# An attention and mixer kernel whose first feed-forward gate runs by token halves, with some loads and thresholds moved

## The chip, the cores and the metric

The kernel runs on one core of a Trainium2 chip. The metric is the device time of one execution in microseconds (us). PE is TensorE, DVE is VectorE, ACT is ScalarE, POOL is GpSimd and SP is SyncE, whose queue issues nearly all DMAs here.

## The reference, cut to what matters

Four batches of 576 tokens go through an attention with 8 heads of 64, a token and channel mixer, and a gated feed-forward layer. All is float32.

```python
scores = (q @ k.T) / 8
scores = where(scores >= max(scores) - tau, scores, -1e9)
attn = softmax(scores) @ v                       # x: (4, 576, 512)
u = x + (relu(x.T @ w_tok1) @ w_tok2).T          # tokens mixed, per channel
x = u + relu(u @ w_ch1) @ w_ch2                  # 512 -> 1536 -> 512
h = relu(x @ w_in)                               # 512 -> 1024
conv[s] = cw[0]*h[s-1] + cw[1]*h[s] + cw[2]*h[s+1]   # along tokens, per channel
out = (h * sigmoid(conv)) @ w_out                # 1024 -> 512
```

## The kernel before, in words

**Stages.** The program starts with `attention(0)` alone. Then, for each batch b, `dense(b)` (the mixer's channel part and the feed-forward layer) is written together with `attention(b + 1)`. Every matmul of the dense part is made of three float16 passes (high by high, low by high, high by low), so each operand exists as a high and a low half, suffixes _h and _l.

**Attention.** A batch has 4 pairs of heads with 9 tiles each, 36 tiles of 128 queries by 576 keys. For each tile PE makes scores (L562, L567 or L571), DVE takes the negated maximum nm (L583), ACT the exponential (L595), DVE masks with the threshold `thr` (L602), ACT makes the float16 high half (L607) and POOL the low half (L611). A DMA on SP then transposes both (L616), and PE multiplies by v (L626, L629; "PV" below). In batch 0 the tiles live in a ring of four places in `act_t`. In batches 0 and 1, where scores are float32, the threshold is made on DVE (L593); in the later ones on POOL. After the 9 tiles of a pair come the normalization (L642 to L655) and the token mixing: first stage L666, second stage L681 and L686, evacuated to the tiles `u` by ACT (L688) and DVE (L689).

**Dense.** L793 is the channel layer up (12 columns f of 128 channels, two token pieces of 256 and 320), L811 the one down, L844 the feed-forward input layer (8 columns f, the same two pieces). The gate of a column follows once both pieces are in `h`: ACT multiplies by the first tap (L827), DVE adds the other two taps (L829, twice), ACT takes a tanh (L831), DVE multiplies (L832), ACT and POOL make the halves of the result in `act_t` (L833, L834). L867 and L870 are the output layer: five token tiles j, each summed over all 8 columns f.

**Weights.** They come as 512-column pieces during attention(0) and dense(0): a load on SP (L347), then POOL (L382), ACT (L385), DVE twice (L386, L388), and ACT and POOL for the halves (L373, L374). `wstep` advances this chain. Its PSUM bank, 4, is handed to the dense part when the last piece (column 7 of w_out) is converted; until then dense(0) has banks 5 and 6, and one output tile j waits for bank 4.

**What sets the order.** All instructions are first recorded in program order; then the class `Order` writes a fixed order for each engine, a list schedule with its own cost figures, which takes the lowest program number among what is ready. Engines and the SP queue then run strictly in that order. Among its rules is `heels`: a load from DRAM that is written after the n-th transposing DMA may not be issued before transpose n-3, as long as n is at most 36, the number of transposes in attention(0).

Of the kernel before, what the change touches and what calls it, by code (L numbers as in the profile page):

```python
# [20 lines left out]
class Order:  # L21
# [4 lines left out]
    def __init__(self, nc, tc, bank_tile, bufs):  # L26
        self.tc, self.bank_tile = tc, bank_tile
        self.group = {n: g for g, names in self.POOLS.items() for n in names}
        self.bufs = bufs
        self.ins = [i for i in nc.cur_bb.bb.instructions if len(i.outs) and self.area(i.outs[0])]  # L30
        n = len(self.ins)
        self.eng = [str(i.engine).split(".")[-1] for i in self.ins]
        self.dma = [i.opcode in ("DMACopy", "DmaTransposeAnt") for i in self.ins]
        self.before, self.first, self.uses, self.turns = [set() for _ in range(n)], [[] for _ in range(n)], [[] for _ in range(n)], {}
        self.depend()
        self.heels, turned = {}, []
        for x, i in enumerate(self.ins):
            if i.opcode == "DmaTransposeAnt":
                turned.append(x)
            elif self.dma[x] and not self.area(i.ins[0])[9] and self.BEHIND < len(turned) <= self.FIRST:  # L40
                self.heels.setdefault(turned[-1 - self.BEHIND], []).append(x)
        self.after = [[] for _ in range(n)]
        for x in range(n):
            for y in self.before[x]:
                self.after[y].append(x)
# [99 lines left out]

    BEHIND, FIRST = 3, 36
    LAP = {"DVE": 85, "Activation": 103, "Pool": 44}
# [102 lines left out]
def kernel(ctx: ExitStack, tc: tile.TileContext, q, k, v, tau,  # L250
# [178 lines left out]
    def load_taps():  # L429
        if conv_w.dtype == F32:  # L430
            nc.sync.dma_start(taps, conv_w)
        else:
# [6 lines left out]
           for i in range(2)]  # L439
    h_t = [const.tile([P, S + 2], F32, name=f"h{i}") for i in range(2)]  # L440
    for t in h_t:
        V.memset(t[:, 0:1], 0.0)
        V.memset(t[:, S + 1:S + 2], 0.0)
    v_t = [(const.tile([P, 2, 2 * NS + 1, D + 2], F16, name=f"vh{i}"),
# [135 lines left out]
    def exps(i):  # L580
# [11 lines left out]
        else:  # L592
            V.tensor_scalar(out=thr, in0=nm, scalar1=-1.0, scalar2=mtaus[:, 0:1], op0=ALU.mult, op1=ALU.add)  # L593
        e = half(i, 0).bitcast(F32) if i < PER else qk2.tile([P, S], F32, tag="x", name="e", bufs=15)
# [156 lines left out]
    def dense(b):  # L751
# [83 lines left out]

        for f in range(NG):
            if b == 0:
                wstep(2)
            for s0, n in SPL:
# [139 lines left out]
```

## Time and profile before

| | |
|---|---|
| median of 3 runs | 770.74 us (770.47 to 771.9) |
| the profiled execution | 770.83 us, its span 769.0 us |
| busy share of the span | PE 95%, DVE 66%, ACT 59%, POOL 54% |
| dense(0)'s first matmul | 114.66 us from the start |
| dense(1)'s first matmul | 304.36 us |

The span runs from the first to the last instruction. All times below are from the span's start. A row's "idle before" names the engine or DMA that ended the wait. Consecutive instructions of one engine overlap by some tens of ns, so a start may lie before the end of the one ahead. The granted clock is 1.0 at 2.4 GHz and 0.5 at 1.2 GHz.

### The profile page before, as it was taken

The page shows a single profiled execution, that of the slowest core. Times are in us where ns is not written, and L with a number is a line of the kernel's source. Part 1 is how long each engine was busy: PE and PEld are TensorE (multiplying, and loading weights), DVE is VectorE, ACT ScalarE, POOL GpSimd, SP SyncE. Part 2 cuts the span into 40 slices and gives each one's busy share as a digit, 9 for nine tenths or more (in the row PEclk, how much of TensorE's full clock was granted, in tenths as well). Part 3 has the DMA queues.
Part 4 walks back from the last instruction along what each step waited for, and adds up shares of the span by engine and source line. Part 5 has one row for each costly group of instructions (what it writes and reads, how often), then busy time and mean ns, then how long its engine had stood idle before and what let it go on. Part 6 is the DMA issues. An engine that isn't in the chain of part 4 may idle for free.

```text
span 769.0 us, 18598 instructions
## 1 busy us (share of the span) xinstructions
PE 726.8 (95%) x7398; PEld 543.3 (71%) x7398; DVE 511.2 (66%) x914; ACT 452.8 (59%) x927; POOL 417.8 (54%) x463
## 2 busy tenths in 40 slices
PE   7889769999998879999999999999999999999998
PEld 4567557777776646788888766778888766788764
DVE  6989768887789961676867952776866941323470
ACT  6977757776768842575657752665656842211471
POOL 5877689887878960466555840366464830000040
PEclk9999979999999999999999999999999999999999
DMA  8999999999997702579777502588863400000001
GB/s 215 224 182 177 265 228 211 240 213 229 204 237 170 156 15 83 122 134 158 159 140 135 86 15 93 114 148 148 153 118 63 78 29 35 1 1 2 1 1 62
DMA packets 200951, 97.00 MB, mean 126 GB/s; under 512 B 174752, under 2 KB 186784, under 8 KB 200864
## 3 DMA queue, kind: packets, MB, share of 16 engines
q1 hardware_dynamic: 200544, 95.55, 59.8%
q8 instruction: 58, 0.95, 0.5%
q10 hardware_dynamic: 320, 0.26, 0.1%
q14 instruction: 29, 0.24, 0.1%
HBM read 39.35 MB, written 4.72 MB: 57 GB/s over the span
## 4 chain that ended last, share of the span: by engine, by line
PE 67%; DVE 9%; DMA 8%; POOL 5%; ACT 5%; issue 4%; SPq 2%; ACTq 0%; POOLq 0%; DVEq 0%
PE ps L811 17%; PE ps L793 15%; PE ps L867 11%; PE ps L844 7%; PE ps L571 4%; PE ps L626 3%; DMA act_t<-act_t 3%; DVE ct L829 3%; PE ps L666 2%; PE ps L681 2%; PE ps L567 2%; PE ps L629 2%; DMA ld<-in_v_dram 1%; POOL ph L611 1%; DVE nm L583 1%
## 5 line engine op out<-in xcount | busy, mean ns | idle before, releaser
L611 POOL TENSOR_TENSOR ph<-e,ph 128x576 f16<-128x576 f32 x108 | 141.6, 1311 | 105.7 <-ACT ph L607 93.5
L811 PE MATMUL ps<-act_t,wc_h 128*128 128x256 f16 (+1 forms) x768 | 149.9, 286 | 0.0
L583 DVE TENSOR_REDUCE nm<-ps 128x1 f32<-128x576 f32 x144 | 107.6, 748 | 20.0 <-PE ps L571 12.8
L602 DVE SCALAR_TENSOR_TENSOR e<-ps,thr,e 128x576 f32<-128x576 f32 x108 | 87.6, 812 | 49.4 <-ACT e L595 41.4
L834 POOL TENSOR_TENSOR act_t<-ct,act_t 128x576 f16<-128x576 f32 x32 | 46.0, 1438 | 132.2 <-ACT act_t L833 130.8
L793 PE MATMUL ps<-u_h,wc_h 128*128 128x320 f16 (+1 forms) x384 | 109.6, 286 | 0.5 <-DVE u_l L689 0.5
L811 PE MATMUL ps<-act_t,wc_l 128*128 128x256 f16 (+1 forms) x384 | 109.7, 286 | 0.0
L793 PE MATMUL ps<-u_h,wc_l 128*128 128x320 f16 (+1 forms) x384 | 109.5, 286 | 0.0
L793 PE MATMUL ps<-u_l,wc_h 128*128 128x320 f16 (+1 forms) x384 | 109.1, 286 | 0.0
L793 PEld LDWEIGHTS <-wc_h 128*128 128x128 f16 x768 | 75.1, 98 | 21.5 <-issue 2.1
L811 PEld LDWEIGHTS <-wc_h 128*128 128x128 f16 x768 | 75.1, 98 | 21.0 <-issue 2.0
L867 PE MATMUL ps<-wo_h,act_t 128*128 128x512 f16 x256 | 77.3, 383 | 4.2 <-ACT h L820 4.2
L829 DVE SCALAR_TENSOR_TENSOR ct<-h,cw,ct 128x576 f32<-128x576 f32 x64 | 71.8, 1125 | 7.5 <-ACT ct L827 7.2
L844 PE MATMUL ps<-u_h,wi_h 128*128 128x256 f16 (+1 forms) x256 | 73.0, 286 | 3.5 <-ACT h L820 1.9
L607 ACT ACTIVATE ph<-e 128x576 f16<-128x576 f32 x108 | 73.1, 677 | 1.2 <-DVE e L602 0.8
L844 PE MATMUL ps<-u_h,wi_l 128*128 128x256 f16 (+1 forms) x256 | 73.1, 286 | 0.0
L844 PE MATMUL ps<-u_l,wi_h 128*128 128x256 f16 (+1 forms) x256 | 73.1, 286 | 0.0
L768 DVE SCALAR_TENSOR_TENSOR act_t<-ps,act_t 128x256 f16<-128x256 f32 x96 | 43.5, 455 | 43.2 <-ACT act_t L767 42.6
L867 PEld LDWEIGHTS <-act_t 128*128 128x128 f16 x384 | 36.9, 98 | 47.2 <-issue 6.4
L626 PE MATMUL ps<-vh,pt 128*128 128x65 f16 (+1 forms) x1080 | 68.8, 195 | 0.6 <-DVE x L646 0.6
L626 PEld LDWEIGHTS <-pt 128*128 128x128 f16 (+1 forms) x1080 | 61.2, 101 | 8.8 <-issue 5.7
L767 ACT ACTIVATE act_t<-ps 128x256 f16<-128x256 f32 x96 | 39.1, 407 | 47.9 <-PE ps L793 47.1
(123 smaller groups left out, 1670.5 us busy)
## 6 DMA issues: line engine op xcount, KB each, us to landing
st<-in_moe_w_ch_dram SPq DMA_DIRECT2D x24, 512.0 KB, 4.6
ld<-in_v_dram SPq DMA_DIRECT2D x32, 160.0 KB, 3.1
kt<-ks SPq DMA_DIRECT2D x32, 144.0 KB, 2.8
st<-in_moe_w_in_dram SPq DMA_DIRECT2D x8, 512.0 KB, 5.0
st<-in_moe_w_out_dram SPq DMA_DIRECT2D x8, 512.0 KB, 4.4
out_dram<-ot SPq DMA_DIRECT2D x16, 256.0 KB, 2.0
kt<-in_k_dram SPq DMA_DIRECT2D x16, 144.0 KB, 4.1
ld<-in_q_dram SPq DMA_DIRECT2D x8, 288.0 KB, 3.6
```

The costliest lines, as they stand in the source:

```text
L583: V.tensor_reduce(out=nm, in_=c["s3"], axis=AX.XY, op=ALU.max, negate=True)
L602: V.scalar_tensor_tensor(out=e3, in0=c["s3"], scalar=c["thr"], in1=e3, op0=ALU.is_ge, op1=ALU.mult)
L607: A.activation(out=c["ph"][:, 0:S], in_=c["e"], func=AF.Copy)
L611: G.tensor_tensor(out=c["ph"][:, S:], in0=c["e"], in1=c["ph"][:, 0:S], op=ALU.subtract)
L626: T.matmul(dst[o:o + m], pt[:, j, o:o + m], vh[:, hh, j, 0:D + 1], start=(j == 0), stop=(j == NSL - 1))
L768: V.scalar_tensor_tensor(out=r_t(f, 1)[:, sl], in0=t, scalar=0.0, in1=r_t(f, 0)[:, sl], op0=ALU.max, op1=ALU.subtract)
L793: T.matmul(t, wc1[wx][:, f, c], u[c][ux][:, sl], start=(c == 0 and i == 0), stop=(c == NC - 1 and i == 2))
L811: T.matmul(t, wc2[wx][:, c, f], r_t(f, rx)[:, sl], start=(by_dve(c) and f == 0 and i == 0), stop=(f == NF - 1 and i == 2))
L829: V.scalar_tensor_tensor(out=ct, in0=ht[:, kk:kk + S], scalar=cw[:, kk, f:f + 1], in1=ct, op0=ALU.mult, op1=ALU.add)
L834: G.tensor_tensor(out=g_t(f, 1), in0=ct, in1=g_t(f, 0), op=ALU.subtract)
L844: T.matmul(t, wi[wx][:, f, c], u[c][ux][:, s0:s0 + n], start=(c == 0 and i == 0), stop=(c == NC - 1 and i == 2))
L867: T.matmul(t, g_t(f, gx)[:, j * P:(j + 1) * P], wo[wx][:, f], **lim)
```

## The change

Three parts. In `dense(0)` alone, the feed-forward input layer and its gate run by halves of the tokens: all 8 columns for tokens 0 to 287, then all 8 for the rest, with two extra tokens per half for the convolution (290 of PSUM's columns instead of 256 and 320). `h` becomes four buffers of a half instead of two of the whole, and two memsets restore the layout for the other batches. Loads that are written after transposes 31 to 36 wait for transpose 36. The threshold of float32 batches is made by ACT.

```diff
-            elif self.dma[x] and not self.area(i.ins[0])[9] and self.BEHIND < len(turned) <= self.FIRST:
-                self.heels.setdefault(turned[-1 - self.BEHIND], []).append(x)
+            elif self.dma[x] and not self.area(i.ins[0])[9] and self.BEHIND < turned <= self.FIRST:
+                heel = turned - 1 - self.BEHIND if turned <= self.LAST else self.FIRST - 1
+                self.heels.setdefault(turns[heel], []).append(x)
...
-    BEHIND, FIRST = 3, 36
+    BEHIND, LAST, FIRST = 3, 30, 36
...
-            V.tensor_scalar(out=thr, in0=nm, scalar1=-1.0, scalar2=mtaus[:, 0:1], op0=ALU.mult, op1=ALU.add)
+            A.activation(out=thr, in_=nm, func=AF.Identity, scale=-1.0, bias=mtaus[:, 0:1])
...
+        def h_half(f, x, t):
+
+            ht = h_t[f % 2][:, (f // 2 + x) % 2 * HW:][:, :HW]
+            A.activation(out=ht[:, 1:HW - 1], in_=t, func=AF.Relu, scale=1.0 / WS2)
+            ct = qk2.tile([P, S], F32, tag="x", name="ct", bufs=15)[:, :hn]
+            A.activation(out=ct, in_=ht[:, 2 * x:2 * x + hn], func=AF.Copy, scale=cw[:, 0, f:f + 1])
+            for kk in (1, 2):
+                V.scalar_tensor_tensor(out=ct, in0=ht[:, 2 * x + kk:2 * x + kk + hn], scalar=cw[:, kk, f:f + 1], in1=ct,
+                                       op0=ALU.mult, op1=ALU.add)
+            A.activation(out=ct, in_=ct, func=AF.Tanh, scale=0.5 / SX)
+            V.scalar_tensor_tensor(out=ct, in0=ct, scalar=1.0, in1=ht[:, 2 * x + 1:2 * x + 1 + hn], op0=ALU.add, op1=ALU.mult)
+            gh, gl = [g_t(f, y)[:, x * hn:(x + 1) * hn] for y in range(2)]
+            A.activation(out=gh, in_=ct, func=AF.Copy)
+            G.tensor_tensor(out=gl, in0=ct, in1=gh, op=ALU.subtract)
...
+        if b == 0:
+            for x in range(2):
+                for f in range(NG):
+                    wstep(1)
+                    bk = dbank()
+                    s0 = x * (hn - 2)
+                    t = ps[:, bk, :hn + 2]
+                    for c in range(NC):
+                        for i, (wx, ux) in enumerate(PASS):
+                            T.matmul(t, wi[wx][:, f, c], u[c][ux][:, s0:s0 + hn + 2],
+                                     start=(c == 0 and i == 0), stop=(c == NC - 1 and i == 2))
+                    flush()
+                    late.append((bk, lambda f=f, x=x, t=t: h_half(f, x, t)))
+                    yield
```

Line numbers behind the change are larger by 2 or 3 up to the gate and by 33 behind it: L616 is then L619, L829 and L832 become L846 and L849 in the halves, L867 is L900.

The first place is the SP queue at the end of attention(0), where `st` is a piece of weights, `ld` is v, and `qt` and `kt` are q and k of a coming pair of batch 1. Before, from the 28th transpose on:

```order
L616 DMA_TRANSPOSE act_t<-act_t 128x9x128 x4
L347 DMA st<-in_moe_w_ch_dram 128x1024
L513 DMA ld<-in_v_dram 128x320 x2
L616 DMA_TRANSPOSE act_t<-act_t 128x9x128 x4
L347 DMA st<-in_moe_w_ch_dram 128x1024
L473 DMA qt_166<-in_q_dram 128x576
L482 DMA kt_0_167<-in_q_dram 64x576
L616 DMA_TRANSPOSE act_t<-act_t 128x9x128
L528 DMA vh_159<-vh_159 64x2x264
L483 DMA kt_1_168<-in_k_dram 64x2x288
L482 DMA kt_0_167<-in_q_dram 64x576
L483 DMA kt_1_168<-in_k_dram 64x2x288
```

After, from the same transpose on:

```order
L619 DMA_TRANSPOSE act_t<-act_t 128x9x128 x9
L349 DMA st<-in_moe_w_ch_dram 128x1024
L516 DMA ld<-in_v_dram 128x320 x2
L349 DMA st<-in_moe_w_ch_dram 128x1024
L476 DMA qt_170<-in_q_dram 128x576
L485 DMA kt_0_171<-in_q_dram 64x576
L486 DMA kt_1_172<-in_k_dram 64x2x288
L485 DMA kt_0_171<-in_q_dram 64x576
L486 DMA kt_1_172<-in_k_dram 64x2x288
L349 DMA st<-in_moe_w_ch_dram 128x1024
```

Six loads that stood among the last nine transposes (two pieces of weights, two of v, one each of q and k) now stand behind the last one, ahead of three more of k and a piece of weights that stood there before too.

The second place is ACT at the last tiles of attention(0); the copies to float16 from `act_t` to `act_t` are those of the tiles (L607, now L610). Before, down to the last tile's copy:

```order
L607 ACTIVATE act_t<-act_t 128x576
L595 ACTIVATE act_t<-ps,nm 128x576
L671 ACTIVATE rh<-ps 128x256
L607 ACTIVATE act_t<-act_t 128x576
L385 ACTIVATE ps<-st 128x512
L595 ACTIVATE e<-ps,nm 128x576
L688 ACTIVATE u_2_h<-ps 128x256
L595 ACTIVATE e<-ps,nm 128x576
L385 ACTIVATE ps<-st 128x512
L607 ACTIVATE act_t<-act_t 128x576
```

After, over the same tiles:

```order
L596 ACTIVATE thr<-nm,mtaus 128x1
L598 ACTIVATE act_t<-ps,nm 128x576
L610 ACTIVATE act_t<-act_t 128x576
L375 ACTIVATE wc_h<-wf 128x512
L596 ACTIVATE thr<-nm,mtaus 128x1
L674 ACTIVATE rh<-ps 128x256
L598 ACTIVATE act_t<-ps,nm 128x576
L610 ACTIVATE act_t<-act_t 128x576 x2
L387 ACTIVATE ps<-st 128x512
L691 ACTIVATE u_2_h<-ps 128x256
L596 ACTIVATE thr<-nm,mtaus 128x1
```

The last two tile copies are now neighbours. Before, two steps of the weights (L385), two exponentials of batch 1 and an evacuation (L688) lay between them. A threshold now stands ahead of exponentials. Further on, the scaling of `kt` for batch 1's second pair (L490, now L493) stands between the two evacuations of the last tile of u; before, it stood ahead of both.

The third place is DVE around the last piece of weights in dense(0); its two steps are the last L386 and L388 (now L388 and L390), `ct` is a gate's work tile and `h_153` and `h_154` are the two `h` tiles. Before:

```order
L388 SCALAR_TENSOR_TENSOR wf<-st,ps 128x512
L829 SCALAR_TENSOR_TENSOR ct<-h_154,cw,ct 128x576
L829 SCALAR_TENSOR_TENSOR ct<-h_153,cw,ct 128x576
L386 SCALAR_TENSOR_TENSOR ps<-st,ps 128x512
L832 SCALAR_TENSOR_TENSOR ct<-ct,h_154 128x576
L388 SCALAR_TENSOR_TENSOR wf<-st,ps 128x512
L829 SCALAR_TENSOR_TENSOR ct<-h_153,cw,ct 128x576
L643 RECIPROCAL rc<-rc 128x5
L583 TENSOR_REDUCE nm<-ps 128x1
L386 SCALAR_TENSOR_TENSOR ps<-st,ps 128x512
L832 SCALAR_TENSOR_TENSOR ct<-ct,h_153 128x576
L388 SCALAR_TENSOR_TENSOR wf<-st,ps 128x512
```

After:

```order
L846 SCALAR_TENSOR_TENSOR ct<-h_153,cw,ct 128x288
L388 SCALAR_TENSOR_TENSOR ps<-st,ps 128x512
L846 SCALAR_TENSOR_TENSOR ct<-h_153,cw,ct 128x288
L390 SCALAR_TENSOR_TENSOR wf<-st,ps 128x512
L649 TENSOR_TENSOR x_3921<-ps,rc 128x4x64
L849 SCALAR_TENSOR_TENSOR ct<-ct,h_153 128x288
L846 SCALAR_TENSOR_TENSOR ct<-h_154,cw,ct 128x288
L652 SCALAR_TENSOR_TENSOR x_3921<-ps,rc,blk 128x128
L388 SCALAR_TENSOR_TENSOR ps<-st,ps 128x512
L846 SCALAR_TENSOR_TENSOR ct<-h_154,cw,ct 128x288
L390 SCALAR_TENSOR_TENSOR wf<-st,ps 128x512
L849 SCALAR_TENSOR_TENSOR ct<-ct,h_154 128x288
```

Behind the last piece's second step stood 3 of the 24 gate operations of 576 columns; now 7 of the 48 of 288 columns stand there. On PE the output layer's first matmuls (L900) now stand ahead of the last two units of the input layer (L863); before, all of the input layer stood ahead of them.

## Rows read from the trace of the kernel before

**Rows 1.** The page: busy tenths of PE and granted clock in 40 slices.

```profile
PE   7889769999998879999999999999999999999998
...
PEclk9999979999999999999999999999999999999999
```

**Rows 2.** Windows of 3 us: length, busy time by engine (count), clock, DMA, GB/s.

```profile
99.00:102.00 3.00, 0.00 (x0) 0.00 (x0) 0.37 (x3) 1.17 (x3) 2.85 (x3) 0.94 1.58 179
...
105.00:108.00 3.00, 2.25 (x19) 1.39 (x20) 2.72 (x6) 1.73 (x4) 1.33 (x3) 0.50 1.11 287
```

**Rows 3.** Timeline of the SP queue: start, length, line, DMA.

```profile
86.42 0.52 SPq L347 DMA_DIRECT2D st<-in_moe_w_ch_dram  x1
86.99 0.90 SPq L513 DMA_DIRECT2D ld<-in_v_dram  x2
...
95.29 0.54 SPq L347 DMA_DIRECT2D st<-in_moe_w_ch_dram  x1
...
97.03 2.23 SPq L616 DMA_TRANSPOSE act_t<-act_t  x1
```

**Rows 4.** The chain that ended last, in order of time: start, length, what.

```profile
97.03 6.74 DMA act_t<-act_t
...
106.99 3.31 PE ps L666 x30
...
114.66 4.25 PE ps L793 x36
...
287.67 1.68 PE ps L666 x30
289.34 10.37 PE ps L867 x48
...
472.26 2.74 PE ps L870 x48
```

**Rows 5.** The page, DMA issues: count, median us to landing.

```profile
act_t<-act_t SPq DMA_TRANSPOSE x36, 3.7
```

**Rows 6.** Timeline of ACT: the last two tile copies of attention(0).

```profile
90.26 0.68 ACT L607 ACTIVATE act_t<-act_t 128x576 f16<-128x576 f32 x1 [1.14 <-DMA act_t<-act_t]
...
94.20 0.68 ACT L607 ACTIVATE act_t<-act_t 128x576 f16<-128x576 f32 x1
```

**Rows 7.** Timeline of POOL: the last low halves of attention(0).

```profile
89.05 3.75 POOL L611 TENSOR_TENSOR act_t<-act_t 128x576 f16<-128x576 f32 x3
...
95.01 1.28 POOL L611 TENSOR_TENSOR act_t<-act_t 128x576 f16<-128x576 f32 x1 [0.44 <-PE ps L629]
```

**Rows 8.** Groups by line over the span: the thresholds, and a like-sized ACT operation.

```profile
L593 DVE TENSOR_SCALAR thr<-nm,mtaus 128x1 f32<-128x1 f32 x72 | 14.6, 204 | 0.4
...
L588 ACT ACTIVATE bias<-nm 128x1 f32<-128x1 f32 x72 | 14.4, 201 | 45.4 <-DVE nm L583 45.0
```

**Rows 9.** Windows in the gate stage of dense(0), columns as in rows 2.

```profile
268.00:272.00 4.00, 0.85 (x7) 0.49 (x5) 4.00 (x5) 0.68 (x1) 3.37 (x3) 1.00 0.06 12
...
228.00:277.00 49.00, 39.70 (x411) 28.51 (x410) 48.37 (x66) 38.66 (x74) 42.64 (x37) 0.97 0.63 134
```

**Rows 10.** Groups by form on DVE from 228 to 277: the gate.

```profile
L829 DVE SCALAR_TENSOR_TENSOR ct<-h,cw,ct 128x576 f32<-128x576 f32 x14 | 19.5, 1396 | 0.0
L832 DVE SCALAR_TENSOR_TENSOR ct<-ct,h 128x576 f32<-128x576 f32 x7 | 8.2, 1168 | 0.0
```

**Rows 11.** Single lines over the span: durations in ns, minimum, median, maximum.

```profile
L829 DVE SCALAR_TENSOR_TENSOR ct<-h,cw,ct x64: 802/874/1920, 232.8 to 747.1; 128x576 f32<-128x576 f32 x64
...
L776 DVE TENSOR_TENSOR us<-us,u_l x18: 424/491/1414, 357.4 to 709.5; 128x256 f32<-128x256 f32 x9, 128x320 f32<-128x320 f32 x9
```

**Rows 12.** Timelines of DVE, ACT and PE: last weight piece, then dense(1)'s start.

```profile
276.11 0.67 DVE L388 SCALAR_TENSOR_TENSOR wf<-st,ps 128x512 int32<-128x512 int32 x1
...
276.82 0.63 ACT L373 ACTIVATE wo_h<-wf 128x512 f16<-128x512 f32 x1
...
304.36 0.27 PE L793 MATMUL ps<-u_h,wc_h 128*128 128x256 f16 x1
```

More of the change, by code (lines that the diff above doesn't have):

```diff
@@ L35, in __init__ @@
         self.depend()
-        self.heels, turned = {}, []
+        self.heels, turned = {}, 0
+        turns = [x for x, i in enumerate(self.ins) if i.opcode == "DmaTransposeAnt"]
         for x, i in enumerate(self.ins):
             if i.opcode == "DmaTransposeAnt":
-                turned.append(x)
-            elif self.dma[x] and not self.area(i.ins[0])[9] and self.BEHIND < len(turned) <= self.FIRST:
-                self.heels.setdefault(turned[-1 - self.BEHIND], []).append(x)
+                turned += 1
+            elif self.dma[x] and not self.area(i.ins[0])[9] and self.BEHIND < turned <= self.FIRST:
+                heel = turned - 1 - self.BEHIND if turned <= self.LAST else self.FIRST - 1
+                self.heels.setdefault(turns[heel], []).append(x)
         self.after = [[] for _ in range(n)]
@@ L439 @@
            for i in range(2)]
-    h_t = [const.tile([P, S + 2], F32, name=f"h{i}") for i in range(2)]
+    HW = S // 2 + 4
+    h_t = [const.tile([P, 2 * HW], F32, name=f"h{i}") for i in range(2)]
     for t in h_t:
-        V.memset(t[:, 0:1], 0.0)
-        V.memset(t[:, S + 1:S + 2], 0.0)
+        for o in (0, HW - 1, HW, 2 * HW - 1):
+            V.memset(t[:, o:o + 1], 0.0)
     v_t = [(const.tile([P, 2, 2 * NS + 1, D + 2], F16, name=f"vh{i}"),
@@ L834, in gate @@
             G.tensor_tensor(out=g_t(f, 1), in0=ct, in1=g_t(f, 0), op=ALU.subtract)
-        for f in range(NG):
-            if b == 0:
-                wstep(2)
+        def h_half(f, x, t):
[25 more added lines that the diff above has]
+                    yield
+            flush()
+            for t in h_t:
+                V.memset(t[:, S + 1:S + 2], 0.0)
+        for f in range(NG if b else 0):
             for s0, n in SPL:
```

## The prediction

> **What bounds the kernel now.** I read the page's slices first. From slice 16 on (about 307 us) PE is busy nine tenths or more of every slice but the last, at full clock [rows 1], so time can be won there only by taking work from PE, which the change does not do; what is won or lost before 307 us is carried to the end. Ahead of that two places stand out. Around 100 us PE does nothing for three microseconds and then runs at half clock [rows 2]. From 228 to 277 us DVE is busy 48.37 of 49 us and POOL 42.64, while PE has only 39.70; between 268 and 272 PE works 0.85 us [rows 9]. The chain of waits names the first cause: the last transpose of attention(0), 6.74 us long, is followed by the first stage of the token mixing and then by dense(0) [rows 4]. In the second place DVE is the bound; the DVE groups show that the gate is most of it, and that it is slow there: 1396 and 1168 ns for operations whose like takes 802 at least [rows 10, 11]. From 114 to 228 us PE is full again [rows 1], so a lead won at 100 us should reach the gate stage.
>
> I make the sum against the profiled execution, 770.8 us (span 769.0), 0.1 above the median of the runs. A change of less than about 0.2%, 1.5 us, can't be told from none.
>
> **The deferred loads.** The last tile's copy on ACT starts 3.9 us after the one before it [rows 6], because five other operations stand between; with the change they are neighbours. Then POOL is next: it is busy until 92.80 with three low halves, and the last follows at once and ends at 94.1 rather than 96.3 [rows 7]. The transpose was also issued 0.7 us after its data were there (97.03 against 96.29), behind loads that now follow it [rows 3]. So it is issued 2.9 us earlier. Its landing took 6.74 us against a median of 3.7 [rows 4, 5], with a piece of weights and two more loads issued just ahead; without them I take the median, 3.0 us less. From there to dense(0)'s first matmul 10.9 us passed (103.77 to 114.66), part of it at half clock: 30 matmuls of the first mixing stage took 3.31 us, where the same 30 take 1.68 at full clock [rows 4]. If PE's idle stretch shrinks from nearly 5 us to about one, the clock should stay up; that is 1.6 us there and, as an estimate for the scores and the second stage in the same stretch, 0.9 more. Sum: 2.9 + 3.0 + 2.5 = 8.4.
>
> A new wait may take part of it. Nine loads, 2.2 MB, now follow the last transpose, and ACT's evacuation of the last u tile stands behind the scaling of the ninth, a piece of k. At the 179 to 287 GB/s of these windows [rows 2] they need 8 to 12 us from about 95, so they land between 103 and 107; with the scaling and evacuation (some 1.5 us) the second half of u is there at 105 to 109, and it is needed a token piece after dense(0) starts at 106.3. I take **8.0 us** won. Least: only the 0.7 and 3.0, 3.7 us. Most: 8.4 plus what the thresholds give.
>
> **The thresholds.** 72 operations of 204 ns leave DVE, 36 in attention(0); an ACT operation of that size takes 201 [rows 8]. Each overlaps its neighbours by about 0.08 us, so 36 are 4.4 us on either engine. DVE is the busier one there, but ACT's exponential now starts later by one such step, and the mask waits for it. I take zero, with 2 us to either side.
>
> **From dense(0) to the gate.** PE starts dense(0) with 28 PV matmuls fewer done than before (the order); 30 slightly wider ones take 1.68 us [rows 4], so about 1.0 comes back later, and 0.5 for late pieces of weights: **+1.5**. The postponed fourth piece was loaded at 86.42 [rows 3] for the fourth column of dense(0), which came some 10 us after 114.66; now it is loaded at about 95 for a column at about 116, still 20 us ahead.
>
> **The gate by halves.** PE's work is the same (192 matmuls of 290 columns for 96 of 256 and 96 of 320). What it buys: output tiles of the first tokens need only first-half gates. But each tile also sums over all columns of w_out, and the last piece of these is converted on DVE among the gates. It was ready on DVE at 276.79 and its high half on ACT at 277.45 [rows 12]. In the changed order, PE has behind it three matmuls of one output tile, a whole tile, the first mixing stage, two tiles, the half tile and the second mixing stage. From [rows 4]: 0.65 + 5.18 + 1.68 + 10.37 + 2.74, and 1.9 for the rest of the way to 304.36 (289.34 + 10.37 + 2.74 = 302.45); in all 22.5 us. Had DVE kept its time, dense(1) would start at 277.45 + 22.5 = 300.0, a gain of 4.4.
>
> DVE does not keep it. Ahead of the last piece's second step stood 14 + 7 gate operations, 27.7 us [rows 10], less 0.08 overlap each, 26.0. Now 41 halves stand there. Undisturbed, one of 288 columns takes about 0.458 us (between 424 and 492 ns for 256 and 320 [rows 11]). The disturbance, averaged over the 21, is 0.52 us above 0.80. Does a half pay it in full? The short operations of the same sort reach 1414 ns, 0.9 above their least, as the long ones do [rows 10, 11]: it goes by operation, not by length. In full: 41 x (0.458 + 0.52 - 0.08) = 36.8, 10.8 us more than now. In proportion to length, 0.26: 26.2, no more than now. POOL's work is spread over a longer stretch, and its operations on the gate are shorter too, so I take 0.38: 31.1, **5.1 us more**. Six thresholds that leave and two small operations that come in about cancel. So 300.0 + 5.1 = 305.1 against 304.36: **+0.8 us**, bounds -4.3 and +6.5.
>
> The Trainium skill, "SBUF — State Buffer", section "Who interferes with whom", says that VectorE operations with two SBUF inputs and GpSimd operations that read SBUF exclude each other for a whole instruction. By that rule the wait does not shrink with the half; the maxima in [rows 11] agree, and the sum by it is the 10.8 us, which makes it the rival "in full" below.
>
> **Sum.** -8.0 + 1.5 + 0.8 = -5.7: 770.8 - 5.7 = **765.1 us**.
>
> **The rivals.** *The disturbance stays in full* (0.52 per operation): the gate stage loses 6.5, 770.8 - 8.0 + 1.5 + 6.5 = 770.8, no change. For it: the maxima of short operations; against it: the same POOL work in a longer stretch. *Slower: gates that follow each other pair off with POOL's*. The half gates stand closer together in DVE's order, and one that starts while POOL holds an operation of 1.3 us waits for most of it. At 0.70 per operation DVE needs 44.2 us, 18.2 more, the stage loses 13.9, and the time is 778.2. It decides from 0.56 on, where the loss of 8.1 and the 1.5 outweigh the lead with 1.5 to spare. For it: the mean of the 14 longer operations is already 0.59 over their least [rows 10, 11]; against it: POOL is not always busy. *The disturbance is in proportion*: the stage gains 4.3, the time is 760.0. For it: shorter POOL operations between; against it: [rows 11]. *The deferral gives little*: POOL's data come no earlier and the clock falls all the same; 3.7 won, 770.8 - 3.7 + 1.5 + 0.8 = 769.4. For it: the nine loads that now gate the last u tile.
>
> **How the numbers follow.** Forecast 0.45, in proportion 0.18, in full 0.10, slower 0.15, little from the deferral 0.12. Faster by over 0.2%: 0.45 + 0.18 + 0.07 of the last, 0.70. Slower: 0.15. Within: the rest, 0.15. The range reaches from 758 (in proportion, with 2 us from the thresholds) to 771 (in full); the slower rival beyond it and the far end below are left out. The forecast's own range is 762 to 768.5.
>
> **What the changed profile would show.** The last transpose issued at about 94 and landed within 4 us; no stretch at half clock around 105; dense(0)'s first matmul at 106 to 107; in the gate stage 48 gate operations with a mean of about 0.84 us; the last weight piece's second DVE step 5 us later relative to dense(0)'s lead; dense(1)'s first matmul at about 298.7. I am wrong if dense(0) starts after 110, if the half gates take 1.0 us or more, or if PE shows new gaps between 115 and 228, where I count on none.

## The result: 0.8% slower, and where the time went

The changed kernel takes 777.09 us (median of 4 runs, 776.09 to 778.28) against 770.61 for the kernel before beside it (769.77 to 771.9): ratio 1.0083, 95% interval 1.0059 to 1.0106. The forecast was 765.1, faster. The profiled execution is 776.1 us (span 774.3) against 770.8.

The page of the kernel after, busy tenths of PE and granted clock, to be laid beside [rows 1]:

```profile
PE   7788779999998789999999999999999999999998
...
PEclk9999999999999899999999999999999999999999
```

Windows of the kernel after: length, busy time by engine (count), clock, DMA share, GB/s.

```profile
99.00:102.00 3.00, 2.18 (x33) 1.28 (x29) 2.83 (x7) 2.65 (x6) 2.83 (x5) 1.00 0.90 295
105.00:108.00 3.00, 2.61 (x28) 1.90 (x29) 2.32 (x5) 1.64 (x6) 2.75 (x6) 1.00 1.07 210
110.00:113.00 3.00, 1.12 (x9) 0.68 (x8) 1.09 (x2) 2.50 (x6) 1.29 (x2) 1.00 0.74 190
268.00:272.00 4.00, 2.00 (x17) 1.34 (x15) 4.00 (x7) 3.35 (x9) 2.77 (x3) 1.00 0.26 53
228.00:277.00 49.00, 37.67 (x363) 27.36 (x360) 47.11 (x71) 37.00 (x87) 36.65 (x38) 0.91 0.57 134
```

Where PE did nothing for three microseconds and then ran at clock 0.50 [rows 2], it now has 2.18 and 2.61 of 3 us at full clock. A new hole stands at 110 to 113 (1.12 of 3). In the gate stage PE is busy 2 us less (37.67 against 39.70) and has done 363 matmuls there instead of 411, at a clock of 0.91 instead of 0.97; DVE is still busy for nearly the whole of it, and POOL is busy 6 us less [rows 9].

The chain that ended last, kernel after, start, length, what:

```profile
97.36 4.67 DMA st<-in_moe_w_ch_dram
102.05 8.37 DMA kt<-in_k_dram
...
283.85 2.66 DVE ct L846 x3
...
286.96 5.56 PE ps L900 x25
292.52 1.68 PE ps L669 x30
294.20 10.37 PE ps L900 x48
```

The transpose that led the chain at 97.03 [rows 4] is gone from it. In its place stands the deferred load of k, and 180 us later three half gates on DVE; behind them stands an evacuation on DVE (L692) for which the output tiles on PE wait. The last two rows of before, at 287.67 and 289.34, come 4.85 us later now, and the distance from there to the end hardly changes. All of the loss is made ahead of 292 us.

The start of dense(0), timelines of SP, ACT and PE in the kernel after (start, length, operation, idle time before it):

```profile
88.31 9.01 SPq L619 DMA_TRANSPOSE act_t<-act_t  x5
...
96.01 1.30 SPq L619 DMA_TRANSPOSE act_t<-act_t  x1
...
102.05 0.78 SPq L486 DMA_DIRECT2D kt<-in_k_dram  x1
```
```profile
110.50 0.77 ACT L493 ACTIVATE kt<-kt,qsc 128x576 f32<-128x576 f32 x1 [1.97 <-DMA kt<-in_k_dram]
111.18 0.42 ACT L691 ACTIVATE u_h<-ps 128x320 f16<-128x320 f32 x1
```
```profile
108.20 0.27 PE L796 MATMUL ps<-u_h,wc_h 128*128 128x256 f16 x1
...
112.18 0.30 PE L796 MATMUL ps<-u_h,wc_h 128*128 128x320 f16 x1 [1.88 <-DVE u_l L692]
```

The last transpose is issued at 96.01, 1.0 us earlier than before, and its data are there at 99.25, 4.5 us earlier. dense(0) starts at 108.20 instead of 114.50 (the 114.66 of [rows 4] is where the chain enters it). Then PE waits 1.88 us for the second half of the last u tile, whose evacuation stands on ACT behind the scaling of the deferred k, which landed at 110.4.

The gate and its end: groups on DVE from 228 to 294 (count, busy us, mean ns), and the timelines of DVE and PE at the last weight piece and at dense(1)'s start.

```profile
L846 DVE SCALAR_TENSOR_TENSOR ct<-h,cw,ct 128x288 f32<-128x288 f32 x32 | 26.8, 850 | 1.1 <-ACT ct L844 1.1
L849 DVE SCALAR_TENSOR_TENSOR ct<-ct,h 128x288 f32<-128x288 f32 x16 | 12.2, 763 | 1.9 <-ACT ct L848 1.8
```
```profile
282.54 0.68 DVE L390 SCALAR_TENSOR_TENSOR wf<-st,ps 128x512 int32<-128x512 int32 x1
```
```profile
309.21 0.27 PE L796 MATMUL ps<-u_h,wc_h 128*128 128x256 f16 x1
```

A half gate operation takes 0.82 us in the mean; 0.84 was forecast. The last piece's second step starts at 282.54, against 276.11 before, and dense(1) at 309.21 against 304.36 [rows 12].

From the start of the token mixing at about 211 us to dense(1), windows of before, of the kernel after, and of two kernels that follow below, halves_alone and deferral_alone:

```profile
212.81:304.36 91.55, 82.25 (x841) 56.81 (x839) 68.42 (x103) 56.37 (x110) 60.10 (x55) 0.98 0.57 132
211.11:309.21 98.10, 85.84 (x840) 59.13 (x839) 73.43 (x121) 61.93 (x143) 57.91 (x63) 0.95 0.54 122
212.08:307.47 95.39, 84.48 (x840) 58.27 (x839) 73.33 (x130) 59.95 (x134) 57.96 (x63) 0.96 0.54 128
209.15:305.84 96.69, 84.01 (x841) 57.53 (x840) 69.51 (x106) 57.26 (x112) 62.06 (x57) 0.96 0.54 129
```

The same 838 matmuls start in each of the four stretches. Of the 6.6 us that the kernel after needs more, PE is idle for 3.0 and busy for 3.6 more. The granted clock explains most of the busy part: 0.95 of 98.1 us where 0.98 of 91.6 were granted, which makes an estimated 3 us of full-speed time that were not granted. In halves_alone 1.6 are idle and 2.2 busy, in deferral_alone 3.4 and 1.8. No run holds the clock fixed, so the two parts aren't separated by an experiment.

Four moments of each profiled execution carry what follows. "Mixing" is the first matmul of the stage of token mixing at about 211 us, "last piece" the start of the last second step of a weight piece on DVE; all are read from the timelines of PE and DVE. The difference is that of the medians of a kernel and of the kernel before on the same chip, in us; the interval is that of the ratio.

| kernel | difference | interval | dense(0) | mixing | last piece | dense(1) |
|---|---|---|---|---|---|---|
| before | | | 114.50 | 212.81 | 276.11 | 304.36 |
| after | +6.5 | 1.0059 to 1.0106 | 108.20 | 211.10 | 282.54 | 309.21 |
| halves_alone | +4.3 | 1.0034 to 1.0068 | 114.34 | 212.08 | 281.04 | 307.47 |
| deferral_alone | +3.1 | 1.0027 to 1.0059 | 108.39 | 209.15 | 279.78 | 305.84 |
| thr_alone | +3.2 | 1.0026 to 1.0051 | 115.98 | 214.26 | 276.18 | 305.51 |
| no_halves | +1.5 | 1.0006 to 1.0033 | 109.86 | 212.82 | 277.16 | 305.47 |
| no_thr | +3.2 | 1.0028 to 1.0056 | 108.84 | 209.98 | 279.68 | 306.36 |
| no_deferral | +8.0 | 1.0091 to 1.0136 | 116.55 | 214.85 | 283.11 | 310.23 |
| lap_84 | +3.4 | 1.0026 to 1.0060 | 114.08 | 213.40 | 275.19 | 307.52 |
| lap_86 | +1.5 | 0.9992 to 1.0026 | 114.08 | 211.85 | 276.21 | 304.82 |
| deferral_keep_qk | +4.7 | 1.0034 to 1.0073 | 110.72 | 211.01 | 282.41 | 308.46 |
| halves_by_column | +3.9 | 1.0037 to 1.0071 | 114.43 | 211.08 | 279.70 | 306.72 |
| halves_weights_first | +4.1 | 1.0051 to 1.0080 | 116.16 | 212.90 | 264.23 | 307.38 |
| halves_deferral_weights_first | +4.8 | 1.0050 to 1.0095 | 109.35 | 210.25 | 267.78 | 308.01 |
| thr_second | +0.9 | 0.9997 to 1.0025 | 114.80 | 212.42 | 274.80 | 304.30 |
| deferral_thr_second | +3.1 | 1.0027 to 1.0068 | 112.05 | 213.88 | 279.55 | 307.86 |
| all_thr_second | +6.7 | 1.0069 to 1.0106 | 109.61 | 211.86 | 283.59 | 310.75 |
| short_dense | -3.9 | 0.9927 to 0.9968 | 112.93 | | 273.36 | 299.09 |
| low_half_by_act | +0.2 | 0.9985 to 1.0018 | 113.19 | 210.06 | 274.15 | 302.02 |
| short_dense_low_half | -7.1 | 0.9902 to 0.9936 | 113.10 | | 268.93 | 296.44 |

Single runs of one kernel lie several us apart (the kernel before: 766.61 to 773.22 over all of its runs; deferral_thr_second: 770.28 to 777.57). The moments belong to one execution each, so a difference of 1 us between two of them says little. That of before took 770.83 us, about 1 us above its medians beside the experiments (769.56 to 770.02), and that of deferral_thr_second 777.27, 4.5 us above its median.

### The profile page after: what moved, and what is told of

It is laid out like the page before. It is cut to its first block, busy times and chain, and to the rows that moved or that the text cites. A ratio compares the mean times of both kernels' runs of the same rounds, so it can differ in the third digit from the quotient of the medians.

```text
span 774.3 us, 18626 instructions
## 1 busy us (share of the span) xinstructions
PE 731.3 (94%) x7398; PEld 544.3 (70%) x7398; DVE 510.4 (66%) x872; ACT 468.7 (61%) x1023; POOL 415.1 (54%) x471
## 4 chain that ended last, share of the span: by engine, by line
PE 63%; DMA 10%; POOL 7%; ACT 7%; DVE 7%; issue 4%; SPq 2%; POOLq 0%; ACTq 0%; DVEq 0%
PE ps L814 18%; PE ps L900 10%; PE ps L796 10%; PE ps L877 5%; DMA act_t<-act_t 4%; PE ps L629 3%; PE ps L574 3%; PE ps L669 3%; POOL ph L614 2%; PE ps L684 2%; PE ps L570 2%; PE ps L632 2%; DMA ld<-in_q_dram 2%; DMA ld<-in_v_dram 1%; DMA st<-in_moe_w_out_dram 1%
## 5 line engine op out<-in xcount | busy, mean ns | idle before, releaser
L837 POOL TENSOR_TENSOR act_t<-ct,act_t 128x576 f16<-128x576 f32 x24 | 34.4, 1432 | 128.4 <-ACT act_t L836 127.0
L900 PE MATMUL ps<-wo_h,act_t 128*128 128x512 f16 x256 | 76.8, 381 | 3.9 <-ACT h L842 3.0
L610 ACT ACTIVATE ph<-e 128x576 f16<-128x576 f32 x108 | 73.0, 676 | 1.0 <-DVE e L605 0.8
L900 PEld LDWEIGHTS <-act_t 128*128 128x128 f16 x384 | 36.8, 98 | 46.0 <-issue 4.8
L877 PE MATMUL ps<-u_h,wi_h 128*128 128x256 f16 (+1 forms) x192 | 54.9, 286 | 1.3 <-ACT h L823 1.0
L877 PE MATMUL ps<-u_l,wi_h 128*128 128x256 f16 (+1 forms) x192 | 54.9, 286 | 0.0
L877 PE MATMUL ps<-u_h,wi_l 128*128 128x256 f16 (+1 forms) x192 | 54.9, 286 | 0.0
L565 PE MATMUL ps<-kt,qt 128*128 128x288 f32 (+1 forms) x160 | 46.8, 450 | 8.3 <-DVE act_t L605 8.2
```

The lines of the kernel that those rows point to most:

```text
L565: T.matmul(s3[o:o + m, a], f32(st["qt"])[:, q0:q0 + m], f32(st["kt"][hh])[:, a * hn:(a + 1) * hn], start=True, stop=True)
L610: A.activation(out=c["ph"][:, 0:S], in_=c["e"], func=AF.Copy)
L877: T.matmul(t, wi[wx][:, f, c], u[c][ux][:, s0:s0 + n], start=(c == 0 and i == 0), stop=(c == NC - 1 and i == 2))
L900: T.matmul(t, g_t(f, gx)[:, j * P:(j + 1) * P], wo[wx][:, f], **lim)
```

## The experiments

### Each edit alone, and the change without each

The kernel before with one of the three edits (halves_alone, deferral_alone, thr_alone), and the kernel after with one taken back (no_halves, no_thr, no_deferral). Taking back the deferral is one number, and taking back the thresholds one line:

```
-    BEHIND, LAST, FIRST = 3, 30, 36
+    BEHIND, LAST, FIRST = 3, 36, 36
...
-            A.activation(out=thr, in_=nm, func=AF.Identity, scale=-1.0, bias=mtaus[:, 0:1])
+            V.tensor_scalar(out=thr, in0=nm, scalar1=-1.0, scalar2=mtaus[:, 0:1], op0=ALU.mult, op1=ALU.add)
```

What was expected of the first four, then of the other two:

> The kernel before with only the gate of the first batch by halves; loads and thresholds as before. Theory A (the halves cost DVE time, and the last piece of w_out comes later): the gate stage loses what it lost in the changed kernel, about 6.5 us, so 776 to 778 us, with the last w_out piece's second DVE step some 5 to 8 us later than the 276.1 of before, and dense(0) at 114.5 as before. Theory B (the halves are about free and the loss comes from the thresholds on ACT): 769 to 772. Theory C (the three edits only hurt together, because a reshuffled order meets another one): 768 to 772 too, but then each edit alone is within 2 us.

> The kernel before with only the late loads moved behind the last transpose of attention(0). Theory A: dense(0) starts about 6 us earlier (108 to 109 instead of 114.5), 1.9 us go to the wait for the second half of the last u tile behind the k load on ACT, and about 2.5 to score and PV matmuls that come back later, so the lead is 1.5 to 2.5 us and the time 768 to 769. The recorded forecast would have 764 to 765. Theory B: the lead lost between 108 and 211 us was the thresholds' doing, so 765 to 767.

> The kernel before with only the float32 thresholds on ACT (72 operations of 0.28 us there instead of 0.20 on DVE). Theory A: in the first 60 us, where PE waits for DVE's masks, the mask waits for the later exponential, and PE is 1.3 us less busy there; all in all 770 to 772. Theory B: the thresholds are the main loss, 774 to 777. If neither, the freed DVE time shows as a gain, 767 to 769.

> The changed kernel with the gate of the first batch whole again; deferral and thresholds stay. Theory A: the gate stage's loss is gone and the lead of 1.7 us at 211 us carries through, 768 to 770. Theory B: still 774 to 777. Theory C: anything else, above all a time that is not the sum of the two single edits.

> The changed kernel with the float32 thresholds back on DVE: halves and deferral stay. If the losses simply add (halves 4, deferral 3, thresholds 3 us against the kernel before, each alone), 776 to 777. If they are new orders of one and the same gate stage, that don't add, 772 to 776. First mixing stage of dense(0)'s tail at about 209 us, as with the deferral alone.

> The changed kernel with the late loads at their old places: halves and thresholds stay. If the losses add, 776 to 777; if they don't, 771 to 775. dense(0) starts at about 116 us, as with the thresholds alone.

Every edit alone is slower, by 3 to 4 us. None of the theories had said so: theory A had the deferral alone ahead. The parts don't add either. Their sum is 10.5, the whole change costs 6.5, and deferral with thresholds (no_halves) only 1.5. With the halves against without them, the cost is 4.3 (alone), 0.2 (beside the deferral), 4.8 (beside the thresholds) and 5.0 (beside both). The deferral costs 3.1 alone and gives back 1.0 to 1.7 beside the others, of the 8 forecast.

The moments are steadier than the times. The deferral does bring dense(0) forward in all four of these kernels that have it, by 4.6 to 6.3 us against before (in deferral_thr_second, below, by 2.5 only, in an execution far above its median). But deferral_alone, 6.1 us ahead at dense(0) and 3.7 at the mixing, is 1.5 us behind at dense(1): the gate stage, from mixing to dense(1), takes 96.7 us there and 91.6 before. The wait for the last u tile isn't the reason: deferral_alone has none of it (ACT scaled that k at 106.83 there, 3.7 us earlier than in the kernel after). PE waits in the gate stage instead; waits of deferral_alone from 212 to 290 us (us in total, times, longest):

```profile
PE ps L846 <- ACT h L822: 7.6, 3, 5.7
PE ps L569 <- DVE e L604: 1.7, 1, 1.7
```

PE needs a bank of PSUM that ACT has still to evacuate into h. Before the longest of these waits ends, that evacuation stands on ACT behind the copy of an earlier column's gate, which waits 3.03 us for DVE; timeline of ACT, then a row of the chain that ended last (L846 is the input layer in this kernel):

```profile
264.58 0.68 ACT L835 ACTIVATE act_t<-ct 128x576 f16<-128x576 f32 x1 [3.03 <-DVE ct L834]
265.17 0.37 ACT L822 ACTIVATE h<-ps 128x256 f32<-128x256 f32 x1
```
```profile
265.59 5.08 PE ps L846 x20
```

PE had waited 5.7 us, and the granted clock is 0.50 while these 20 matmuls run. They take 5.08 us; at full clock 36 of like size take 4.25 [rows 4], so the lower clock costs about 2.7 us here, as an estimate, on the chain.

### Another order, the same work

One constant of the planner's cost model is changed in the kernel before (lap_84, and lap_86 to the other side). No instruction comes or goes.

```
-    LAP = {"DVE": 85, "Activation": 103, "Pool": 44}
+    LAP = {"DVE": 84, "Activation": 103, "Pool": 44}
```

> A placebo: the kernel before with one constant of its planner changed, the time it reckons a DVE operation to overlap the next, from 85 to 84 ns. No work is added or taken away, only the order that the planner writes changes, as it does after every edit. Theory C (the kernel before is an order tuned by hand, and any new order of the gate stage costs some us): slower by 1.5 to 4 us, with dense(1) later by as much and the loss in the gate stage. Theory A and B (the edits themselves cost): within 1 us of before.

> The same placebo to the other side, 86 ns instead of 85. Theory C: slower by 1 to 4 us. Theories A and B: within 1 us of before.

84 costs 3.4 us, as much as an edit; 86 can't be told from none. Theory C holds in so far that an order alone can cost what one edit does. In lap_84 it is made in the gate stage too: 94.1 us from mixing to dense(1). Windows of lap_84:

```profile
240.00:272.00 32.00, 25.73 (x288) 19.72 (x287) 32.00 (x44) 24.22 (x49) 31.75 (x27) 1.00 0.61 122
272.00:290.00 18.00, 15.33 (x113) 8.41 (x113) 9.46 (x16) 8.47 (x17) 9.92 (x9) 0.81 0.04 15
```

DVE and POOL are full up to 272, and PE then has 2.7 us of idle time and a clock of 0.81. So a loss of 3 us after a single edit is no proof of that edit's own cost; only what recurs in several kernels, or shows in the moments, can be put down to it.

### Does a lead get through the gate stage?

short_dense leaves one of three passes (low half of the weights by high half of u) out of dense(0)'s first layer, so its output is less precise:

```
                     for i, (wx, ux) in enumerate(PASS):
+                        if b == 0 and i == 1:
+                            continue
```

> The kernel before, without the second of the three passes (low half of the weights by high half of u) of dense(0)'s first layer: 96 matmuls of 256 or 320 columns less, about 11.6 us of TensorE's time, so its output is less precise; every operation on DVE, ACT and POOL stays. It gives the gate stage a lead that no reordering has to find. If a lead at 211 us carries through the gate stage, as the forecast took it, dense(1) starts 9 to 11 us earlier and the time is 759 to 761. If the gate stage is bound by the work of POOL and DVE and by the loads of w_out, whenever TensorE gets there, most of it is lost there: 765 to 769.

Of 11.6 us less work on PE, 9.3 are there at the first matmul of the gate's input layer (216.69 against 225.96; dense(0) had started 1.6 earlier), 5.3 at dense(1), and 3.9 in the median. The lead does not get through. The windows of 228 to 272 us, first of short_dense, then of before, and the waits of short_dense in the stage:

```profile
228.00:272.00 44.00, 34.83 (x379) 25.14 (x378) 42.02 (x60) 34.12 (x67) 43.76 (x39) 0.92 0.57 140
```
```profile
228.00:272.00 44.00, 35.73 (x398) 26.97 (x397) 43.42 (x59) 34.15 (x64) 39.09 (x33) 1.00 0.70 149
```
```profile
PE ps L846 <- ACT h L822: 8.1, 4, 3.7
```

POOL has become full (43.76 of 44), DVE nearly so, and PE waits 8.1 us for the same evacuation. Earlier work on PE runs into engines that have no more room.

low_half_by_act takes work from POOL: the low half of each gate of the first batch is a scaled copy by ACT (and not the low half).

```
-            G.tensor_tensor(out=g_t(f, 1), in0=ct, in1=g_t(f, 0), op=ALU.subtract)
+            if b:
+                G.tensor_tensor(out=g_t(f, 1), in0=ct, in1=g_t(f, 0), op=ALU.subtract)
+            else:
+                A.activation(out=g_t(f, 1), in_=ct, func=AF.Copy, scale=2.0 ** -13)
```

> The kernel before, with the low half of each gate of the first batch written by ACT, as a scaled copy, and not by POOL as the difference (eight operations of 1.48 us leave POOL, and its result is not the low half): this takes work from POOL and with it the waits of DVE's gate operations on POOL, and adds eight copies of about 0.7 us to ACT. If POOL with DVE is the bound of the gate stage, the mean of DVE's first gate operations falls from 1.40 to 1.1 us or less, the last weight piece comes 4 to 8 us earlier, and the time is 763 to 767. If not, 768 to 772.

The time stays. DVE's first gate operations fall to 1238 ns from 1396 only, and POOL's busy time from 39.09 to 29.71 of 44 us; now PE waits for attention(1)'s transposes instead:

```profile
PE ps L626 <- DMA pt<-ph: 4.5, 1, 4.5
```

The way from mixing to dense(1) takes 92.0 us, 91.6 before. POOL alone is thus not the bound either. Both probes in one:

> Both probes in one: the kernel before without one pass of dense(0)'s first layer (765.7 by itself) and with the gate's low halves as ACT copies in place of POOL's differences (769.7 by itself); both results are less precise. If the gate stage is held by TensorE's late arrival and by POOL in turn, each hiding the other, the two together give more than their sum: 758 to 762. If it is held by something that neither touches (DVE, the loads of w_out, the order), about their sum or less: 764 to 767.

7.1 us, where the two medians add to 3.7. That speaks for two limits that hide each other. In the profiled executions the gains at dense(1) are 5.3, 2.3 and together 7.9, which is about the sum; but low_half_by_act had its 2.3 at the mixing already. Counted from the first matmul of the gate's input layer to dense(1), the stage takes 78.4 us before, 82.4 in short_dense, 78.8 in low_half_by_act and 78.9 with both: of a lead of 8.4 us at its start (217.53) only 0.5 are lost in it, where short_dense lost 4.0 of 9.3. So in these executions a lead gets through once POOL's gate work, and with it a part of DVE's waits for POOL, is gone. The other 3 us of the 11.6 are lost ahead of the stage.

### Which loads were deferred

deferral_keep_qk lets only weights and v wait for the last transpose; q and k keep their places (the edit against deferral_alone).

```
-                heel = turned - 1 - self.BEHIND if turned <= self.LAST else self.FIRST - 1
+                heel = self.FIRST - 1 if turned > self.LAST and self.area(i.outs[0])[0][:2] not in ("qt", "kt") else turned - 1 - self.BEHIND
```

> The deferral alone, but the loads of q and k for the next attention keep their places; only weights and v wait for the last transpose. If the scaling of the late k on ACT, ahead of the last u tile, is what held dense(0) up, that wait of about 1.9 us at 111 us is gone, but one or two of these loads stand ahead of the last transpose again, so dense(0) starts at 108 to 110. The first mixing stage at 211 us comes at 208 to 209. Theory A says the lead is then kept and the time is 767 to 769; theory C says that the gate stage swallows it as it did with the whole deferral (7 us more from the mixing at 209 us to the last weight piece than before), 771 to 774.

dense(0) starts at 110.72. PE still waits 1.4 us for a u tile, so earlier k loads don't end that wait. From mixing to dense(1) 97.5 us pass, the most of the kernels with whole gates. The gate stage swallows the lead, as theory C had it.

### What in the halves costs

Both start from halves_alone. halves_by_column runs both halves of a column one after the other; halves_weights_first keeps the order of the halves but puts all of the weights' last conversion steps among the first halves. halves_deferral_weights_first is the latter with the deferral.

```
-            for x in range(2):
-                for f in range(NG):
+            for f in range(NG):
+                for x in range(2):
                     wstep(1)
...
-                    wstep(1)
+                    wstep(2 - 2 * x)
```

> The halves alone, but column by column: both halves of a column one after the other, as the whole gates were, with the same 48 half operations on DVE. If the cost of the halves is in the operations themselves (5.7 us more from the mixing at 212 us to the last weight piece), dense(1) starts at 309 to 311 and the time is 775 to 778, since the early output tiles are lost as well. If it is the order of the halves (first all first halves) that costs, it is back at 769 to 772.

> The halves alone, with the last sixteen steps of the weights' conversion all among the first halves of the gate (two to a unit), and none among the second. If the halves lose because the last piece of w_out waits on DVE behind the second halves' operations (281.0 us there, 276.1 in the kernel before), that piece is ready some 6 to 9 us earlier, at 272 to 275, and the time is back at 767 to 770. If the stage is held elsewhere (the second halves themselves, attention(1), loads), dense(1) stays at 306 to 308 and the time at 773 to 775.

> The same with the deferral too. By the first theory the lead of the deferral would be kept as well, 764 to 767; by the other one, 771 to 774, like halves and deferral without the earlier conversion (772.8).

halves_by_column is as slow as halves_alone (3.9 and 4.3), so the order of the halves is not it, though dense(1) did not come to 309 either: losing the early tiles costs nothing that shows. Converting early moves the last piece from 281.04 to 264.23 and leaves dense(1) where it was, 307.38 against 307.47. The place of the last piece, on which the forecast hung the gate stage, does not set its end. Window and waits of halves_weights_first:

```profile
240.00:256.00 16.00, 6.58 (x58) 4.55 (x57) 16.00 (x26) 12.33 (x27) 14.82 (x17) 0.88 0.77 179
```
```profile
PE ps L629 <- DVE x L649: 5.2, 1, 5.2
PE ps L570 <- DVE e L605: 4.3, 2, 3.0
```

With DVE full (16.00 of 16), the conversions that come forward push attention(1)'s operations back, and PE waits for those. It looks as if the whole sum on DVE has to be worked off, whatever stands first: in halves_alone DVE is busy 42.96 of the 44 us up to 272, and it goes on with gates to 286. That is a reading; no run takes work from DVE alone. With the deferral, halves_deferral_weights_first is 4.8 us slower than before: no lead is kept.

Eight kernels of the table have the halves and can be compared with one that lacks only them. The halves cost 3.6 to 5.0 us in six of these pairs, and 0.2 and 1.7 in the two whose other kernel is deferral_alone. Six costs above what another order of the same work moved (3.4) make the halves the best shown part of the loss.

### Where the thresholds lose

thr_second puts the thresholds on ACT in attention(1) alone; deferral_thr_second adds the deferral to that, and all_thr_second is the whole change with the thresholds of attention(0) back on DVE.

```
+            (A.activation(out=thr, in_=nm, func=AF.Identity, scale=-1.0, bias=mtaus[:, 0:1]) if i >= PER else
             V.tensor_scalar(out=thr, in0=nm, scalar1=-1.0, scalar2=mtaus[:, 0:1], op0=ALU.mult, op1=ALU.add))
```

> The thresholds on ACT in attention(1) alone; in attention(0) they stay on DVE. If the loss of the thresholds (3.2 us alone) comes from attention(0), where the exponential behind each is later and PE waits for the masks, it is gone: dense(0) at 114 to 115 and 768 to 771. If it comes from the gate stage, 772 to 774.

> A candidate: the deferral, and the thresholds on ACT in attention(1) alone; whole gates. dense(0) at 108 to 109, as with the deferral alone. If attention(0) was all that the thresholds lost by, and the freed DVE time (some 7 us of small operations between 114 and 277 us) lets a part of the lead through the gate stage, 766 to 769; if the gate stage swallows the lead again, 770 to 773.

> The whole change, but with the thresholds of attention(0) back on DVE. If the thresholds' loss is in attention(0), 772 to 775, some 3 us less than the changed kernel (777.1); if it is in the gate stage, 776 to 778.

Alone the loss can't be told from none without attention(0) (0.9 instead of 3.2, dense(0) at 114.80 instead of 115.98). The operation itself, as a single line of the kernel after (minimum, median, maximum), and PE's waits for masks up to 116 us in thr_alone and in before:

```profile
L596 ACT ACTIVATE thr<-nm,mtaus x72: 278/286/297, 8.1 to 253.2; 128x1 f32<-128x1 f32 x72
```
```profile
PE ps L564 <- DVE act_t L604: 7.9, 9, 2.3
```
```profile
PE ps L562 <- DVE act_t L602: 6.2, 10, 1.8
```

It takes 286 ns on ACT, not the 201 of the row that I took for it [rows 8]. PE waits 7.9 us for masks, 6.2 before; but in deferral_alone, with the thresholds on DVE, it is 8.2 up to dense(0), so this wait isn't shown to be the way in which the time is lost. In the whole change, moreover, taking the thresholds out of attention(0) gives nothing (6.7 against 6.5), and deferral_thr_second is no better than the deferral alone. The place of the loss is thus shown for the edit by itself and not for the sum.

## Why the prediction was wrong

At dense(1) the forecast was 5.7 us ahead of before, and 4.9 behind were measured. Of these 10.6 us, 1.7 were missed ahead of dense(0), 3.1 from there to the mixing, and 5.8 from the mixing to dense(1), in the term of the gate by halves.

**The step that failed** in the first two is "a lead won at 100 us should reach the gate stage", and the sum that then counted it in full up to the end. Of the 8.0 forecast, 6.3 came at dense(0): the term for the earlier issue of the last transpose, 2.9, measured 1.0, since POOL's last low half ended at 95.81, not 94.1; the landing gave 3.5 for 3.0, and the way from there to dense(0) 1.8 for 2.5. At the mixing 1.7 were left. 1.9 went to the last u tile, which I had named as a possible wait but priced at 0.4 (its k landed at 110.4, not by 107); as waits of before are gone, PE's idle time on the way grows by 0.9. Its busy time grows by 3.7 (100.60 against 96.92 us), for 28 PV and six score matmuls that were no longer done ahead of dense(0); +1.5 was set down, and the six scores were overlooked. deferral_alone kept 3.7 at the mixing and still lost all of it. short_dense points to the stage and not the deferral: of a lead of 9.3 us at its start, made for the most part by work left out, 5.3 are left at its end. I had read DVE as the bound of that stage and yet added a gain of PE's ahead of it to the total.

**The gate by halves**, the largest miss, was to cost 0.8, and from mixing to dense(1) the kernel after needs 6.6 more, halves_alone 3.8. The disturbance of an operation was sized about rightly: 0.82 us per half where 0.84 was taken. DVE's last piece comes 5.7 us later after the mixing in halves_alone (5.1 forecast) and 8.1 in the kernel after. The other side of the term, a gain of 4.4 behind the last piece, came out at 1.8 and 1.6 (28.25 us from last piece to dense(1) before, 26.43 and 26.67 now). Seven half operations of the gate are still to be done on DVE after the last piece, and the evacuation for which the output tiles wait stands behind them in part (2.66 us of the chain, of which PE is idle for 0.93). halves_weights_first shows that the piece was the wrong thing to follow. The sum also priced every matmul of the stage at full clock; that the clock falls where PE waits, and the same matmuls then take longer (3.6 us in the kernel after, most of it by the clock), was in none of its terms.

**The rivals.** "In full" gave nearly the loss of the gate stage (6.5 forecast, 6.6 measured) but for another reason, since the price per operation stayed that of the forecast: a match by luck. "Pair off" did not come, 0.82 is far from 1.0, and that its 778.2 lies near the 777.1 measured is luck too. "The deferral gives little" was nearest in what it gave, but not in how: the clock stayed up at 105, the lead is there at dense(0), and it is lost behind it.

**The thresholds**, set at 0 with 2 to either side, cost 3.2 by themselves, at or near attention(0).

Of the signs that I had named, no half clock at 105, dense(0) before 110, half gates under 1.0 and no new gap behind 115 (PE is busy 97.58 of 98 us from 114 to 212) held; the last transpose at about 94 did not (96.01), nor dense(0) at 106 to 107. None of those that were to prove me wrong looked at the place that decided it.

What stays open is how the 6.5 us divide. An unchanged program in another order costs up to 3.4 us here, edits in pairs give 1.5 to 8.0, and no experiment separates the last two microseconds of an edit from the order that the planner found for it, or the waits of the gate stage from the clock that falls with them. None of these kernels with the full result beats the kernel before.

## What to carry to other kernels

Before a gain is added to the end, follow it through the next stage in which the engine that gains is not the bound: time won for TensorE ahead of a stage that DVE and POOL fill is turned into waits there, and a probe that leaves out work ahead of it shows how much gets through. Waits in such a stage were dearer than their idle time here, because the granted clock fell with them. In a program whose order a planner writes, run the same work in one or two other orders first; here that moved the time by up to 0.4%, and a smaller effect of one edit can't be read from one kernel. Cutting an operation in two on a full engine costs its fixed part once more (0.49 us undisturbed for a half gate, 0.79 for a whole) and a good part of its wait (0.33 and 0.51 in the mean); moving what waits behind it changed which wait was seen here, not the end.

## What the chip showed that was not expected

DVE's gate operation waits for the end of a POOL operation, to some hundredths of a microsecond. Timelines of POOL and DVE, kernel before, then POOL and DVE, kernel after:

```profile
237.74 1.67 POOL L374 TENSOR_TENSOR wo_l<-wf,wo_h 128x512 f16<-128x512 f32 x1
...
240.50 1.28 POOL L611 TENSOR_TENSOR ph<-e,ph 128x576 f16<-128x576 f32 x1
```
```profile
238.44 1.59 DVE L829 SCALAR_TENSOR_TENSOR ct<-h,cw,ct 128x576 f32<-128x576 f32 x1
...
240.62 1.78 DVE L829 SCALAR_TENSOR_TENSOR ct<-h,cw,ct 128x576 f32<-128x576 f32 x1
```
```profile
248.18 0.73 POOL L852 TENSOR_TENSOR act_t<-ct,act_t 128x288 f16<-128x288 f32 x1
248.87 1.50 POOL L614 TENSOR_TENSOR ph<-e,ph 128x576 f16<-128x576 f32 x1
```
```profile
248.24 0.99 DVE L846 SCALAR_TENSOR_TENSOR ct<-h,cw,ct 128x288 f32<-128x288 f32 x1
249.15 1.53 DVE L849 SCALAR_TENSOR_TENSOR ct<-ct,h 128x288 f32<-128x288 f32 x1
```

The whole operation ends 0.62 us after the POOL operation that was running when it started (240.03 against 239.41, 242.40 against 241.78), the half 0.32 and 0.31 after it (249.23 against 248.91, 250.68 against 250.37), whatever was left of POOL's. Of the 24 whole operations of dense(0), 21 began while POOL was running one, and each of them ends 0.60 to 0.62 us after it. Operations that found POOL idle take 0.44 to 0.52 us for a half. The Trainium skill, "SBUF — State Buffer", section "Who interferes with whom", states that such operations exclude each other, and these rows agree with it for DVE as the second to come: it waits to the end of the first. The step from the rule to a price was what could go wrong: the mean excess of a half, 0.82 less 0.49 undisturbed, is 0.33 us and not the 0.51 of a whole (1.30 in the mean less 0.79). What made it fall was not tested; POOL's own gate operations are shorter (847 ns in the mean against 1457), and 19 of the 48 halves found no wait, against 6 of the 24 wholes.
